# An attention, expert and feed-forward kernel on one core: the first token tile meets the first two experts by itself

## The chip, the core and the metric

The kernel is one program on one NeuronCore of a Trainium2 chip. TensorE (PE) multiplies matrices, VectorE (DVE), ScalarE (ACT) and GpSimd (POOL) do the rest, SyncE (SP) issues nearly all transfers. The metric is the time of one execution on the device in microseconds (us); less is better. The median of three runs before is 1221.71 us (1219.14 to 1221.81).

## What is computed

```python
def _attn_ref(q, k, v):                      # 2 x 8 heads, 576 positions, 64 wide
    scores = scale * np.matmul(q, k.transpose(0, 1, 3, 2))
    kth = np.partition(scores, -top_k, axis=-1)[..., -top_k:-top_k + 1]   # top_k = 32
    mask = scores >= kth
    ...
    return np.matmul(attn, v)

def _moe_ref(x, w_gate, w1, w2):             # 1152 tokens x 512, 8 experts, 1024 wide
    logits = x @ w_gate
    ...                                      # P: eight rounds of row and column sums over all tokens
    for e in range(E):
        h = np.maximum(x @ w1[e], 0.0)
        ye = h @ w2[e]
        out += P[:, e:e + 1] * ye

def _moe2_ref(x, w_in, w_out):               # 512 -> 2048 -> 512
    h = x @ w_in
    ...                                      # g = h * tanh(softplus(h))
    return g @ w_out
```

Attention gives 1152 tokens of 512 numbers; eight experts take every token, weighted by a gate that is normalised over all tokens; a last feed-forward part follows.

## The kernel before

**Tiles.** The tokens are nine tiles of 128 (t = 0 to 8). A unit of attention is one tile and one of its eight heads (t, h), so there are 72. The experts take the tiles in three chunks, `CHUNKS = [(0, 1), (2, 3), (4, 5, 6, 7, 8)]`. A pass (`ffn_pass`) is one expert on one chunk; it goes through eight pieces of the expert's weights (128 of the 1024 hidden columns each).

**Precision.** The experts' matmuls run on the rounded kind of float fp32r. Weights and tokens are split into a rounded part and the rest (`wh`, `wl`; `xh`, `xl`; `hh`, `hl`), and each product is three fp32r matmuls. For a piece, `load_piece` brings two 128x512 blocks (`wraw0`, `wraw1`, three buffers each), ACT rounds them and POOL (or DVE, later) subtracts. First matmuls `h` (12 for a chunk of two tiles, 256 columns each) go to PSUM under the tag `mm1` with two buffers; ACT makes `hh` from it, DVE makes `hl`, and both have to be done before the buffer is used again, so the `h` of piece f+2 waits for the `hl` of piece f. Second matmuls `y` (three of 512 columns for each tile) follow two pieces later (`LAG`).

**Attention unit.** PE makes scores `sc`, ACT copies them to `s`; DVE finds the 32nd largest number with four MAX8 (`top`) and three MATCH_REPLACE8 (`w`); ACT takes the exponential, DVE masks it and sums (`em`, `sm`; for the first 13 units POOL shares in that), DVE makes the reciprocal `r`, ACT scales `em`; PE transposes it (`tr`, `tr2`) and multiplies by the values (`pv`, once for two heads). When a tile is done its sums become `xh` and `xl`. Scores of tiles 2 and 3 and half of 5 and 6 are made early (`EARLY`) and kept in buffers or in DRAM (`away`).

**Order.** PE's order is written out by hand: the program runs generators, and what they yield in turn is PE's order. `attention()` runs alone until tile 1 is done. Then `moe_chunk(0)` and `moe_chunk(1)` are stepped (a step is one `h` or one `y` group), and attention advances by `RATE` units for each step after the first `HOLD`. After that chunk 2 and the last part run with PE alone to wait for. The order of the other engines is made by a scheduler at build time from priorities and stays fixed: each engine takes its instructions strictly in that order. The first MAX8 of each head of tile 2 is held behind the last reciprocal of tile 1:

```python
if i == 0 and t == CHUNKS[0][-1] + 1:
    if "ends" in live:
        after(top8, live["ends"])
```

Results of chunks 0 and 1 cannot be weighted before the gate is known, so `spill` copies `y` to SBUF (`ysp`, ACT and DVE in turn) and to DRAM.

## Time and profile before

| | |
|---|---|
| median of three runs | 1221.71 us |
| profiled execution | 1221.39 us |
| its span, first to last instruction | 1219.6 us |
| PE busy | 1168.7 us (96%) |
| DVE busy | 854.7 us (70%) |
| ACT / POOL busy | 660.2 us / 540.8 us |
| first matmul of the experts | 108.25 us |
| last head's transposes on PE | 521.16 us |
| first matmul of chunk 2 | 561.82 us |

1.8 us of the profiled execution lie outside its span. Ends of matmuls are modelled and matmuls overlap, so the rate of PE is read from the starts of matmuls that follow each other, not from their durations. The same holds for DVE, where the next instruction starts some 0.08 us before the one ahead is shown to end.

### The profile page before, as it was taken

Reading aid. Unit: us, or ns where it says so; the run is one execution under the profiler, and the core shown is the slowest. Engines: PE = TensorE matmul, PEld = TensorE weight load, DVE = VectorE, ACT = ScalarE, POOL = GpSimd, SP = SyncE. Lnnn points to the kernel's source line nnn. Section 1 sums busy time; section 2 is a strip of 40 time slices with the busy share of each in tenths; the row PEclk is TensorE's granted clock in tenths of the full one; section 3 lists DMA queues with packets and bytes.
Section 4 is the critical chain, followed back from the end, with each engine's and each line's share of the span. In section 5 each row is a group of like instructions: output and inputs, shape, how many; then the busy total and the mean of one; then the engine's idle time right before and its main releaser. Section 6 shows DMA issues by size and latency. Waiting matters only on the chain.

```text
span 1219.6 us, 21194 instructions
## 1 busy us (share of the span) xinstructions
PE 1168.7 (96%) x7459; PEld 1048.4 (86%) x7459; DVE 854.7 (70%) x1873; ACT 660.2 (54%) x1321; POOL 540.8 (44%) x424
## 2 busy tenths in 40 slices
PE   2677999999999999999999999999999999999998
PEld 2566888998989899899999999999999999999997
DVE  7999999999999999713656868677666633433221
ACT  6786777877777778654223333333333334554432
POOL 7844778877777877774112112121121122221210
PEclk9899999999999999999999999999999999999999
DMA  8434565576655555665235665656445332223201
GB/s 258 126 129 152 171 178 170 170 224 188 211 163 168 157 162 164 186 220 169 70 89 180 199 190 176 207 178 192 138 134 160 119 98 64 93 95 114 78 26 44
DMA packets 105114, 183.20 MB, mean 150 GB/s; under 512 B 14128, under 2 KB 24624, under 8 KB 105008
## 3 DMA queue, kind: packets, MB, share of 16 engines
q1 hardware_dynamic: 103712, 180.68, 47.6%
q8 instruction: 58, 0.95, 0.3%
q10 hardware_dynamic: 1296, 1.18, 0.3%
q14 instruction: 48, 0.39, 0.1%
HBM read 158.55 MB, written 23.27 MB: 149 GB/s over the span
## 4 chain that ended last, share of the span: by engine, by line
PE 86%; DVE 11%; DMA 1%; ACT 1%; issue 0%; POOL 0%; SPq 0%; POOLq 0%; ACTq 0%
PE h_c2e L619 18%; PE y_c2e L596 18%; PE h_d L619 8%; PE y_d L596 8%; PE y_c0e L596 7%; PE h_c0e L619 7%; PE h_c1e L619 6%; PE y_c1e L596 6%; DVE top L254 4%; DVE w L261 4%; PE pv L348 2%; PE tr L325 2%; PE sc L226 2%; PE pv L355 1%; DVE em L290 1%; DMA wraw_c0e<-in_wst_dram 1%
## 5 line engine op out<-in xcount | busy, mean ns | idle before, releaser
L522 POOL TENSOR_TENSOR wl_c2e<-wraw_c2e,wh_c2e 128x512 fp32r<-128x512 f32 x64 | 84.2, 1315 | 341.2 <-ACT wh_c2e L520 326.5
L522 POOL TENSOR_TENSOR wl_c0e<-wraw_c0e,wh_c0e 128x512 fp32r<-128x512 f32 x128 | 171.6, 1356 | 53.1 <-ACT wh_c0e L520 50.9
L522 POOL TENSOR_TENSOR wl_c1e<-wraw_c1e,wh_c1e 128x512 fp32r<-128x512 f32 x128 | 173.3, 1371 | 48.6 <-ACT wh_c1e L520 45.2
L520 ACT ACTIVATE wh_c2e<-wraw_c2e 128x512 fp32r<-128x512 f32 x128 | 80.8, 632 | 186.9 <-PE y_c2e L596 95.0
L254 DVE MAX8 top<-w 128x8 f32<-128x576 f32 x216 | 157.8, 747 | 0.8
L619 PE MATMUL h_c2e<-xh,wh_c2e 128*128 128x256 f32 (+1 forms) x512 | 158.3, 309 | 0.0
L619 PE MATMUL h_c2e<-xl,wh_c2e 128*128 128x256 f32 (+1 forms) x512 | 158.0, 309 | 0.0
L619 PE MATMUL h_c2e<-xh,wl_c2e 128*128 128x256 f32 (+1 forms) x512 | 157.8, 308 | 0.0
L538 DVE SCALAR_TENSOR_TENSOR hl_c2e<-h_c2e,hh_c2e 128x256 fp32r<-128x256 f32 (+1 forms) x128 | 62.5, 488 | 99.7 <-ACT hh_c2e L537 99.3
L596 PE MATMUL y_c2e<-wh_c2e,hh_c2e 128*128 128x512 f32 x320 | 126.0, 394 | 0.0
L596 PE MATMUL y_c2e<-wl_c2e,hh_c2e 128*128 128x512 f32 x320 | 125.9, 394 | 0.0
L596 PE MATMUL y_c2e<-wh_c2e,hl_c2e 128*128 128x512 f32 x320 | 125.2, 391 | 0.0
L522 POOL TENSOR_TENSOR wl_d<-wraw_d,wh_d 128x512 fp32r<-128x512 f32 x32 | 41.5, 1297 | 160.2 <-ACT wh_d L520 160.2
L520 ACT ACTIVATE wh_c0e<-wraw_c0e 128x512 fp32r<-128x512 f32 x128 | 80.5, 629 | 52.9 <-PE y_c0e L596 21.0
L261 DVE MATCH_REPLACE8 w<-top,w 128x576 f32<-128x576 f32 x144 | 106.4, 740 | 0.0
L557 DVE TENSOR_TENSOR hl_d<-mg_d,hh_d 128x256 fp32r<-128x256 f32 x64 | 38.5, 602 | 91.7 <-ACT hh_d L556 91.7
L520 ACT ACTIVATE wh_c1e<-wraw_c1e 128x512 fp32r<-128x512 f32 x128 | 80.3, 629 | 40.4 <-PE y_c1e L596 16.4
L619 PEld LDWEIGHTS h_c2e<-xh,wh_c2e 128*128 128x128 f32 x512 | 96.2, 188 | 2.5
L619 PEld LDWEIGHTS h_c2e<-xl,wh_c2e 128*128 128x128 f32 x512 | 96.1, 188 | 2.3
L619 PEld LDWEIGHTS h_c2e<-xh,wl_c2e 128*128 128x128 f32 x512 | 96.8, 189 | 0.0
L226 PE MATMUL sc<-ks,q 128*128 128x288 f32 x320 | 63.1, 330 | 26.0 <-ACT early L239 8.2
L537 ACT ACTIVATE hh_c2e<-h_c2e 128x256 fp32r<-128x256 f32 (+1 forms) x128 | 54.8, 428 | 55.3 <-PE h_c2e L619 53.0
(170 smaller groups left out, 3352.8 us busy)
## 6 DMA issues: line engine op xcount, KB each, us to landing
wraw_c0e<-in_wst_dram SPq DMA_DIRECT2D x128, 256.0 KB, 3.0
wraw_c1e<-in_wst_dram SPq DMA_DIRECT2D x128, 256.0 KB, 3.0
wraw_c2e<-in_wst_dram SPq DMA_DIRECT2D x128, 256.0 KB, 3.0
cx<-in_w_dram SPq DMA_DIRECT2D x32, 512.0 KB, 4.2
wraw_d<-w SPq DMA_DIRECT2D x64, 256.0 KB, 2.6
yd<-ysp SPq DMA_DIRECT2D x32, 256.0 KB, 3.6
yb<-yd SPq DMA_DIRECT2D x32, 256.0 KB, 3.2
w<-cc SPq DMA_DIRECT2D x32, 256.0 KB, 3.5
```

What stands on the lines that cost most here:

```text
L226: nc.tensor.matmul(halves[half], q[:, h % HG, :], ks[b, h][:, half * HS : (half + 1) * HS], start=(i == 0), stop=(i == len(terms) - 1),)
L254: top8 = nc.vector.max(g, src)
L261: nc.vector.match_replace(w, g, src, NEG)
L325: nc.tensor.transpose(tr[:, c, :], em[:, j * D + c * P :][:, :P], ident)
L348: nc.tensor.matmul(pv[i * D : (i + 1) * D, pair, c0:c1], vmain[b, pair][:, i, c, :], live["at", i][:, c, c0:c1], start=(c == 0), stop=False,)
L520: nc.scalar.activation(hi, raw, AF.Copy)
L522: eng.tensor_sub(lo, raw, hi)
L537: nc.scalar.activation(h, ps, AF.Relu)
L538: live["hl"] = nc.vector.scalar_tensor_tensor(l, ps, 0.0, h, op0=ALU.max, op1=ALU.subtract)
L557: nc.vector.tensor_sub(l, g, h)
L596: nc.tensor.matmul(y, h[:, j * P : (j + 1) * P], w, start=(f == 0 and k == 0), stop=(f == nf - 1 and k == 2),)
L619: nc.tensor.matmul(ps, w[:, c * P : (c + 1) * P], x[:, c, c0 : c0 + m], start=(k == 0), stop=(k == 3 * NC - 1),)
```

## The change

Tile 0 and experts 0 and 1 are taken out of the passes of chunk 0. A new generator, `alone(0, e)`, multiplies tile 0 by the unsplit weights in full precision (plain 32-bit floats, `wraw0` and `wraw1` straight from the transfer, no rounding, no subtraction): for a piece, four matmuls `h_a` of 128 columns, one ReLU on ACT, one matmul `y_a` of 512 columns. It is stepped beside tile 1's attention, from the moment at which tile 0 is done, at 4.8 steps for each unit. Chunk 0 and chunk 1 then run experts 2 to 7 as before, and two passes of the three tiles 1, 2 and 3 (384 columns) take experts 0 and 1 at the end of chunk 1 (`LateRelu`); the third tile's `y` stands in the PSUM tile of the scores (`sc`). `xh` and `xl` of chunks 0 and 1 become one tile each, so two early scores that lay there go to DRAM too (16 in place of 14). Tile 1's transposes use one PSUM bank in place of two. `RATE` becomes 0.29.

```diff
--- before.py
+++ after.py
@@ -47,7 +47,8 @@
 POOL_UNITS = 13
 EARLY = [(t, h) for t in (2, 3) for h in range(H)] + [(t, h) for t in (5, 6) for h in range(HG)]
 EARLY_FROM, EARLY_PER_STEP = 5, 2
-HOLD, RATE = 8, 0.25
+HOLD, RATE = 8, 0.29
+ALONE, ALONE_RATE = 2, 4.8
 FILL_FROM = 11
 
 
@@ -126,18 +127,23 @@
     xh, xl = {}, {}
 
     def x_tiles(i):
         if i not in xh:
-            xp = xlast if i == len(CHUNKS) - 1 else xfirst
-            n = P * len(CHUNKS[i])
-            xh[i] = xp.tile([P, NC, n], F32R, name=f"xh{i}", tag=f"xh{i}")
-            xl[i] = xp.tile([P, NC, n], F32R, name=f"xl{i}", tag=f"xl{i}")
+            ends = i == len(CHUNKS) - 1
+            xp, tiles = (xlast, CHUNKS[-1]) if ends else (xfirst, CHUNKS[0] + CHUNKS[1])
+            both = [xp.tile([P, NC, P * len(tiles)], F32R, name=f"{k}{i}", tag=f"{k}{i}") for k in ("xh", "xl")]
+            for j in [i] if ends else (0, 1):
+                at = P * tiles.index(CHUNKS[j][0])
+                xh[j], xl[j] = (x[:, :, at : at + P * len(CHUNKS[j])] for x in both)
+            if not ends:
+                xh["late"], xl["late"] = (x[:, :, P:] for x in both)
         return xh[i], xl[i]
 
     place = {t: (i, j) for i, c in enumerate(CHUNKS) for j, t in enumerate(c)}
 
     def groups(n):
 
-        return [(0, n)] if n <= 256 else [(0, 256), (256, n - 256)]
+        return [(0, n)] if n <= 384 else [(0, 256), (256, n - 256)]
 
     ps_b = wq = None
 
@@ -307,7 +313,7 @@
 
     def turned(t, i, name):
 
-        if t <= CHUNKS[0][-1] and i % 2:
+        if t < CHUNKS[0][-1] and i % 2:
             bank = ps_m.tile([P, 512], F32, tag="mm2", name=name, bufs=2)
         else:
             bank = ps_a.tile([P, 512], F32, tag="tr", name=name)
@@ -362,6 +368,10 @@
                     nc.scalar.activation(hi, pv[:, pair, :], AF.Copy)
                     nc.vector.tensor_sub(lo, pv[:, pair, :], hi)
             elif h == H - 1:
+                if t == 0:
+                    live["x"] = yp.tile([P, NC, P], F32, tag="ysp", name="x_alone")
+                    with st("first"):
+                        nc.scalar.activation(live["x"], pv, AF.Copy)
                 hi, lo = (x[:, :, i * P : (i + 1) * P] for x in x_tiles(ci))
                 nc.scalar.activation(hi, pv, AF.Copy)
                 nc.vector.tensor_sub(lo, pv, hi)
@@ -428,18 +438,16 @@
         def early(t, h):
 
             k = EARLY.index((t, h))
-            if k < 2:
-                x = xfirst.tile([P, S], F32, tag=("xh1", "xl1")[k], name=f"early{k}")
-            elif k < 10:
-                name = ("xh2", "xl2")[(k - 2) // 4]
-                if (k - 2) % 4 == 0:
+            if k < 8:
+                name = ("xh2", "xl2")[k // 4]
+                if k % 4 == 0:
                     stores[name] = xlast.tile([P, 4, S], F32, tag=name, name=f"early_{name}")
-                x = stores[name][:, (k - 2) % 4, :]
+                x = stores[name][:, k % 4, :]
             else:
                 with st("attn"):
                     x = sp.tile([P, S], F32, tag="away", name=f"early{k}", bufs=2)
             yield from scores(t, h, x)
-            if k >= 10:
+            if k >= 8:
                 with st("attn"):
                     away[t, h] = dram.tile([P, S], F32, tag=f"away_{t}_{h}", name=f"away_{t}_{h}")
                     nc.sync.dma_start(away[t, h], live.pop(("s", t, h)))
@@ -539,6 +547,23 @@
 
         later = ()
 
+    class LateRelu(Relu):
+        def __init__(self, name, n):
+            self.hh = qp.tile([P, n], F32R, tag="q1", name=f"hh_{name}", bufs=3)
+            self.hl = qp.tile([P, n], F32R, tag="q2", name=f"hl_{name}", bufs=3)
+    class Plain:
+        lag = 1
+        def __init__(self, name):
+            self.h = hp.tile([P, P], F32, tag="hh", name=f"h_{name}")
+        later = ()
     class Mish:
 
 
@@ -590,7 +615,10 @@
         def second(f, act, w2):
             with st("moe"):
                 if f == 0:
-                    ys.extend(bank2(f"y_{tag}_{t}") for t in tiles)
+                    third = ps_b is None and len(tiles) > 2
+                    ys.extend(bank2(f"y_{tag}_{t}") for t in tiles[: 2 if third else None])
+                    if third:
+                        ys.append(ps_a.tile([P, 2, 512], F32, tag="sc", name=f"y_{tag}_{tiles[2]}")[:, 0, :])
                 for j, y in enumerate(ys):
                     for k, (h, w) in enumerate(((act.hh, w2[0]), (act.hh, w2[1]), (act.hl, w2[0]))):
                         nc.tensor.matmul(
@@ -651,22 +679,71 @@
         spilled.append((t, e, d))
 
     def moe_chunk(ci):
-        for e in range(E):
+        rounds = [(e, CHUNKS[ci], x_tiles(ci), Relu) for e in range(ALONE if ci < 2 else 0, E)]
+        if ci == 1:
+            tiles = (CHUNKS[0] + CHUNKS[1])[1:]
+            rounds += [(e, tiles, (xh["late"], xl["late"]), LateRelu) for e in range(ALONE)]
+        for e, tiles, x, act_class in rounds:
             put = spill if ci in SPILLED else combine
             yield from ffn_pass(
                 f"c{ci}e{e}",
-                CHUNKS[ci],
+                tiles,
                 [wst[p] for p in range(e * EP, (e + 1) * EP)],
-                *x_tiles(ci),
-                Relu,
+                *x,
+                act_class,
                 lambda t, y, e=e, put=put: put(t, e, y),
             )
 
+    def alone(t, e):
+        ys = []
+        def second(f, act, w2):
+            with st("moe"):
+                if f == 0:
+                    ys.append(bank2(f"y_a{e}_{t}"))
+                nc.tensor.matmul(ys[0], act.h, w2, start=(f == 0), stop=(f == EP - 1))
+            if f == EP - 1:
+                with st("evict"):
+                    spill(t, e, ys[0])
+        for f in range(EP):
+            p = wst[e * EP + f]
+            with st("moe"):
+                raw = []
+                for a in range(2):
+                    raw.append(wp.tile([P, DM], F32, tag=f"wraw{a}", name=f"wraw{a}_a{e}_{f}", bufs=3))
+                    nc.sync.dma_start(raw[a], p[:, a * DM : (a + 1) * DM])
+                ps = ps_m.tile([P, 512], F32, tag="mm1", name=f"h_a{e}_{f}", bufs=2)[:, :P]
+                for c in range(NC):
+                    nc.tensor.matmul(
+                        ps, raw[0][:, c * P : (c + 1) * P], live["x"][:, c, :], start=(c == 0), stop=(c == NC - 1)
+                    )
+            act = Plain(f"a{e}_{f}")
+            with st("first"):
+                nc.scalar.activation(act.h, ps, AF.Relu)
+            yield
+            pending.append(Job(act, partial(second, f, act, raw[1])))
+            while len(pending) > pending[0].act.lag:
+                pending.pop(0).second()
+                yield
 
     at = attention()
-    for _ in at:
+    apart = chain(*(alone(0, e) for e in range(ALONE)), flush())
+    done, since = 0, None
+    for pos in at:
+        if "done" in live:
+            since = since or pos
+            while done < ALONE_RATE * (pos - since):
+                next(apart, None)
+                done += 1
         if live.get("done") == CHUNKS[0][-1]:
             break
+    for _ in apart:
+        pass
     mo = chain(moe_chunk(0), moe_chunk(1), flush())
     begin = pos = CHUNKS[0][-1] * H + H + AHEAD + 2
     for i, _ in enumerate(mo):
```

The built programs show what this does to the order. First, PE beside tile 1's attention, where names are tile and head (`sc_1_6` is scores of tile 1, head 6; `pv_1` the value sums of tile 1; `y_a0_0` and `h_a0_3` are expert 0 on tile 0). Before, from the scores of head 6 to those of head 7:

```order
L226 MATMUL sc_1_6_880<-ks_0_6_241,q2_1_1_0_593 128x288
L325 MATMUL tr_1_1_906<-ident_102,em_1_0_681 128x128 x4
L336 MATMUL tr2_1_1_913<-ident_102,em_1_0_681 128x128
...
L355 MATMUL pv_1_917<-at2_1_1_915,vt_0_0_154 128x128
...
L226 MATMUL sc_1_7_951<-ks_0_7_278,q2_1_1_0_593 128x288
L325 MATMUL tr_1_2_982<-ident_102,em_1_2_835 128x128 x4
```

And now:

```order
L232 MATMUL sc_1_6_922<-ks_0_6_241,q2_1_1_0_597 128x288
L721 MATMUL h_a0_3_933<-x_alone_796,wraw0_a0_3_929 128x128 x4
L331 MATMUL tr_1_1_959<-ident_102,em_1_0_685 128x128 x4
L707 MATMUL y_a0_0_853<-wraw1_a0_2_884,h_a0_2_891 128x512
L721 MATMUL h_a0_4_971<-x_alone_796,wraw0_a0_4_967 128x128 x4
L342 MATMUL tr2_1_1_978<-ident_102,em_1_0_685 128x128
L707 MATMUL y_a0_0_853<-wraw1_a0_3_931,h_a0_3_938 128x512
...
L361 MATMUL pv_1_983<-at2_1_1_980,vt_0_0_154 128x128
L721 MATMUL h_a0_5_999<-x_alone_796,wraw0_a0_5_995 128x128 x4
...
L232 MATMUL sc_1_7_1028<-ks_0_7_278,q2_1_1_0_597 128x288
L707 MATMUL y_a0_0_853<-wraw1_a0_4_969,h_a0_4_976 128x512
L721 MATMUL h_a0_6_1040<-x_alone_796,wraw0_a0_6_1036 128x128 x4
```

The value sums of the first pair and the scores of head 7 now stand behind first and second matmuls of six and five pieces of expert 0, counted from the end of tile 0.

Second, DVE after the last reciprocal of tile 1 (`r_1_7`), up to the first `hl` of the experts. Before:

```order
L300 RECIPROCAL r_1_7_1142<-r_1_7_1142 128x1
L254 MAX top_2_0_1127<-early0_321 128x8
L254 MAX top_2_1_1153<-early1_330 128x8
...
L363 TENSOR_TENSOR xl0_793<-pv_1_917,xh0_792 128x128
L261 MATCH_REPLACE w_2_0_1128<-top_2_0_1127,w_2_0_1128 128x576
L261 MATCH_REPLACE w_2_1_1154<-top_2_1_1153,w_2_1_1154 128x576
L254 MAX top_2_0_1127<-w_2_0_1128 128x8
L538 SCALAR_TENSOR_TENSOR hl_c0e0_0_1208<-h_c0e0_0_0_1209,hh_c0e0_0_1207 128x256
```

And now:

```order
L306 RECIPROCAL r_1_7_1308<-r_1_7_1308 128x1
L260 MAX top_2_0_1293<-early_xh2_321 128x8
L260 MAX top_2_1_1331<-early_xh2_321 128x8
...
L296 SCALAR_TENSOR_TENSOR em_2_0_1345,sm_2_0_1344<-early_xh2_321,top_2_0_1293,e_2_0_1302 128x576
L676 COPY ysp_0_1_1384<-y_a1_0_1194 128x512
L369 TENSOR_TENSOR xl0_799<-pv_1_983,xh0_798 128x128
...
L305 TENSOR_SCALAR r_2_2_1724<-sm_2_2_1721 128x1
L260 MAX top_2_6_2008<-early_xl2_453 128x8
L546 SCALAR_TENSOR_TENSOR hl_c0e2_0_1416<-h_c0e2_0_0_1417,hh_c0e2_0_1415 128x256
```

Before, 16 rows stand between the two; now 52: 19 MAX8, 14 MATCH_REPLACE8, four masks, one spill copy, three `xl` and eleven small ones. From the `xl` of tile 0 to `r_1_7` there were 17 MAX8, 12 MATCH_REPLACE8, two compares and four `xl`; now there are 18, 15, three and two.

Third, DVE where the heads of tile 4 begin (tiles 0 to 3 have their scores early or are done). Before:

```order
L538 SCALAR_TENSOR_TENSOR hl_c0e3_6_2721<-h_c0e3_6_0_2722,hh_c0e3_6_2720 128x256
L254 MAX top_3_6_2760<-w_3_6_2761 128x8
L254 MAX top_3_7_2867<-w_3_7_2868 128x8
L254 MAX top_4_0_3041<-s_4_0_2746 128x8
L290 SCALAR_TENSOR_TENSOR em_3_6_2881,sm_3_6_2880<-s_3_6_2525,top_3_6_2760,e_3_6_2769 128x576
L290 SCALAR_TENSOR_TENSOR em_3_6_2881,sm_3_7_3054<-s_3_7_2561,top_3_7_2867,e_3_7_2876 128x576
L261 MATCH_REPLACE w_4_0_3042<-top_4_0_3041,s_4_0_2746 128x576
```

And now:

```order
L305 TENSOR_SCALAR r_3_6_2953<-sm_3_6_2950 128x1
L305 TENSOR_SCALAR r_3_7_3116<-sm_3_7_3114 128x1
L306 RECIPROCAL r_3_6_2953<-r_3_6_2953 128x1
L306 RECIPROCAL r_3_7_3116<-r_3_7_3116 128x1
L546 SCALAR_TENSOR_TENSOR hl_c0e5_0_2698<-h_c0e5_0_0_2699,hh_c0e5_0_2697 128x256
L546 SCALAR_TENSOR_TENSOR hl_c0e5_1_2733<-h_c0e5_1_0_2734,hh_c0e5_1_2732 128x256
L676 COPY ysp_1_4_2763<-y_c0e4_1_2350 128x512
L546 SCALAR_TENSOR_TENSOR hl_c0e5_2_2780<-h_c0e5_2_0_2781,hh_c0e5_2_2779 128x256
L260 MAX top_4_0_3101<-s_4_0_2822 128x8
```

Before, the first head of tile 4 lies among work of tile 3; now three `hl` and a copy stand ahead of it with no attention between them. On PE the scores `sc_4_0` stand where they stood, between the transposes of heads 3 and 4 of tile 3; DVE now has all of tile 3 behind it by then, where before two masks of tile 3 came after.

## Rows read from the trace of the kernel before

**Rows 1.** The page: busy time of two engines, and 40 slices of the span.

```profile
PE 1168.7 (96%) x7459; PEld 1048.4 (86%) x7459; DVE 854.7 (70%) x1873; ACT 660.2 (54%) x1321; POOL 540.8 (44%) x424
...
PE   2677999999999999999999999999999999999998
...
DVE  7999999999999999713656868677666633433221
```

**Rows 2.** The page: the chain that ended last, shares by engine.

```profile
PE 86%; DVE 11%; DMA 1%; ACT 1%; issue 0%; POOL 0%; SPq 0%; POOLq 0%; ACTq 0%
```

**Rows 3.** Busy time by stretch: PE, PEld, DVE, ACT, POOL, clock, DMA share, GB/s.

```profile
76.50:108.25 31.75, 22.32 (x163) 17.44 (x162) 31.68 (x86) 25.68 (x60) 10.91 (x10) 0.95 0.55 174
104.50:509.10 404.60, 400.69 (x2980) 358.41 (x2981) 397.72 (x972) 304.06 (x592) 313.55 (x234) 1.00 0.57 175
540.00:560.00 20.00, 20.00 (x131) 18.12 (x130) 6.01 (x12) 11.93 (x24) 17.73 (x15) 1.00 0.78 239
```

**Rows 4.** DVE, then PE, in order of time: last head of attention, then chunk 2.

```profile
507.94 0.82 DVE L290 SCALAR_TENSOR_TENSOR em<-s,top,e 128x576 f32<-128x576 f32 x1
...
508.99 0.17 DVE L300 RECIPROCAL r<-r 128x1 f32<-128x1 f32 x1
...
519.33 0.60 PE L325 MATMUL tr<-ident,em 128*128 128x128 f32 x4
519.69 0.48 PE L596 MATMUL y_c1e<-wh_c1e,hh_c1e 128*128 128x512 f32 x1
...
521.16 0.60 PE L325 MATMUL tr<-ident,em 128*128 128x128 f32 x4
...
561.82 0.28 PE L619 MATMUL h_c2e<-xh,wh_c2e 128*128 128x256 f32 x1
```

**Rows 5.** PE in order of time, a `y` group, an `h` group, the next `y`.

```profile
117.22 0.39 PE L596 MATMUL y_c0e<-wh_c0e,hh_c0e 128*128 128x512 f32 x1
...
118.59 0.28 PE L619 MATMUL h_c0e<-xh,wh_c0e 128*128 128x256 f32 x1
...
119.98 0.39 PE L596 MATMUL y_c0e<-wh_c0e,hh_c0e 128*128 128x512 f32 x1
```

**Rows 6.** The chain in order of time, chunk 2: 12 `h` of 256 columns, 12 of 384.

```profile
615.71 3.53 PE h_c2e L619 x24
```

**Rows 7.** PE in order of time: end of tile 0's, then of tile 1's attention.

```profile
76.23 0.49 PE L355 MATMUL pv<-at,vt 128*128 128x128 f32 x2
...
108.00 0.49 PE L355 MATMUL pv<-at,vt 128*128 128x128 f32 x2
108.25 0.36 PE L619 MATMUL h_c0e<-xh,wh_c0e 128*128 128x256 f32 x1
```

**Rows 8.** ACT's copies of 128x128, all: count | busy us, mean ns | idle before.

```profile
L339 ACT ACTIVATE at<-tr 128x128 f32<-128x128 f32 x36 | 9.6, 268 | 0.0
```

**Rows 9.** Transfers between 76 and 109 us.

```profile
DMA packets 4948, 5.56 MB, mean 168 GB/s; under 512 B 2384, under 2 KB 2896, under 8 KB 4944
```

**Rows 10.** DVE in order of time: from tile 0's end to the first `hl`.

```profile
78.90 0.67 DVE L367 TENSOR_TENSOR xl<-pv,xh 128x512 fp32r<-128x512 f32 x1
...
104.47 0.16 DVE L300 RECIPROCAL r<-r 128x1 f32<-128x1 f32 x1
104.55 1.40 DVE L254 MAX8 top<-early 128x8 f32<-128x576 f32 x2
105.86 1.40 DVE L254 MAX8 top<-early_xh 128x8 f32<-128x576 f32 x2
107.18 0.07 DVE L261 MATCH_VALUE_LOAD w<-top,early 128x8 f32 x1
107.24 0.74 DVE L261 MATCH_REPLACE8 w<-top,early 128x576 f32<-128x576 f32 x1
107.90 0.14 DVE L271 TENSOR_SCALAR nb<-top 128x1 f32<-128x1 f32 x1
...
112.51 0.40 DVE L538 SCALAR_TENSOR_TENSOR hl_c0e<-h_c0e,hh_c0e 128x256 fp32r<-128x256 f32 x1
```

**Rows 11.** DVE's `hl` (L538) alone, in the long stretch of attention.

```profile
104.50:509.10 404.60, 45.39 (x111) 1.00 0.57 175
```

**Rows 12.** The mask's line: count, shortest, median and longest duration in ns.

```profile
L290 DVE SCALAR_TENSOR_TENSOR em<-s,top,e x49: 798/865/1891, 95.5 to 507.9; 128x576 f32<-128x576 f32 x49
```

**Rows 13.** Groups of instructions: DVE's MAX8 on scores, and what it waited for.

```profile
L254 DVE MAX8 top<-s 128x8 f32<-128x576 f32 x62 | 46.5, 750 | 6.0 <-ACT s L235 5.7 <-DMA s<-away 0.2
```

## The prediction

> **What bounds the kernel now.** I read the page first. PE is busy in nine tenths or more of every slice from the fifth on, and DVE in nine tenths or more of slices 2 to 15 [rows 1]. The chain that ended last gives PE 86% and DVE 11% [rows 2]: one engine nearly throughout, and the other ahead of it. Two stretches settle what that means [rows 3]. Between 104.5 and 509.1 us, from the first MAX8 of tile 2 to the last reciprocal, DVE is busy 397.7 of 404.6 us and PE 400.7: both are full, so neither has room to take work from the other's shortage. From 540 us on PE is full and DVE busy 6 of 20. Third, the ends [rows 4]: DVE is through with attention at 509.2 us, PE makes the last transposes at 521.2 and begins chunk 2 at 561.8. So DVE is 10 us ahead at that point, and PE sets the end. Before 108.25 us it is the other way: between 76.5 and 108.25 DVE is busy 31.7 of 31.75 us, PE at most 22.3 [rows 3]. The gap there is what the change wants to fill.
>
> All sums below are made against the profiled execution: 1221.39 us, span 1219.6, 1.8 outside. The median of the runs is 1221.71, 0.3 above. I take 0.3% (3.7 us) as what a measurement here can tell from no change.
>
> **What the change takes out.** A `y` group of two tiles lasts 1.37 us and an `h` group of 256 columns 1.39, start to start [rows 5], so a two-tile piece costs 2.76. In chunk 2 the 24 `h` of 256 and 384 columns last 3.53 [rows 6], which leaves 2.14 for 384 columns; nine `y` at 0.228 are 2.06, so a three-tile piece costs 4.20. Out go 32 two-tile pieces (88.3 us), in come 16 three-tile ones (67.2): **21.1 us less PE work** behind the start of the experts. The 384-column form gains nothing by itself. What is saved is tile 0's share.
>
> **What it adds beside tile 1.** Per piece four plain 32-bit matmuls of 128 columns and one of 512. The trace has the first: `pv` of 128x128 (two records) starts at 108.00 and the next matmul at 108.25 [rows 7], 0.25 us. The 512-column one it does not have: at least 0.23 us (the fp32r form), at most four times 0.25; I take 1.0, since it is the same kind of number. A piece is 2.0 us (1.2 to 2.0), 16 are 32 us (20 to 32). The Trainium skill's page FP8 and Floating Point Precision, TensorE Precision Notes, says that true FP32 takes four passes through the array. No run here shows that for 512 columns; by it the `y_a` would be 4 x 0.228 = 0.91 us and the 16 pieces 30.6 us.
>
> Tile 1's own PE work there is at most 22.3 us [rows 3], and less, since ends are modelled; I take 18. Tile 0 ends at 76.5 [rows 7], so the experts' split passes can start on PE at 76.5 + 18 + 32 = 126.5, with some waits **128** (117 with the low price, 140 if nothing overlaps), against 108.25. On ACT come 16 copies of 128x128 (0.27 us each [rows 8]) and two larger ones, 5.5 us on top of 25.7 busy [rows 3]: covered, because the stretch grows to some 50 us. If it were not covered, it would cost those 5.5 us. The transfers: 5.56 MB were moved in that stretch [rows 9], and 13 more pieces of 0.52 MB after three preloaded ones make 12.4 MB; at 239 GB/s, the rate of a full stretch [rows 3], 52 us, to 128.5. That is just hidden by PE's own 128; two more early scores to DRAM are in that noise. SP issues in order, and some of the weights stand behind fetches of scores that wait for a buffer which a mask of tile 1 frees, so they can't run ahead of DVE.
>
> **What it moves on DVE, which decides.** DVE's order from tile 0's `xl` to the last reciprocal of tile 1 took 78.90 to 104.63 us without a pause [rows 10]. The new order has one MAX8 (0.655 each, from the starts at 104.55 and 105.86), three MATCH_REPLACE8 with their load (0.72, 107.18 to 107.90) and a compare (under 0.7) more there, and two small `xl` fewer: 3.0 us, because the `xl` of tile 0 now comes sooner in the order and still has to wait for the same PE work. So tile 2 begins on DVE at **107.6** (104.6 if that slack is found elsewhere, 115 if the 11 us of new PE work ahead of head 7's scores are not covered by the 9 us in which PE idled).
>
> Then 52 rows stand ahead of the first `hl`: 19 x 0.655 + 14 x 0.72 + 4 masks of 0.8 + some 2 = 27.7 us, to 135.3. Before it was 112.5. The third `h` group waits for that `hl` and stands 2.8 us behind the first, so PE in effect starts at 132.9, not at 128: a shift of 24.7 us against 21.1 saved, **+3.6 us** from this alone. What is late next is every `y` behind it.
>
> **The DVE sum.** From tile 2 on DVE has the same 56 heads. Its 397.7 us fall by eleven `hl` (111 [rows 11] against 100 by the same head, at 0.41 less 0.08 of overlap), less 0.6 for four wider ones, and by one copy of 0.6: 3.6. The masks: shortest 0.80 us, median 0.87, longest 1.89 [rows 12], so something holds them up. POOL is busy 313.6 of these 404.6 us [rows 3]. The Trainium skill's page SBUF — State Buffer, SBUF: two separate sides, says that DVE and GpSimd share a port pair, and a DVE operation with two SBUF inputs and a GpSimd one that reads SBUF shut each other out for a whole instruction. The spread of the masks agrees; that POOL causes it is not shown by the rows. With a tenth fewer subtractions in the stretch the masks might lose a tenth of their excess, 1.5 us (0 to 14, if all ran at their shortest). So DVE needs 392.6 us.
>
> Idle time: 6.9 us before, of which MAX8 on fresh scores waited 5.7 over the whole kernel [rows 13]. DVE's 158 rows from that first `hl` to `top_4_0` sum to 80 us, to 215; PE's work from the third `h` to the end of `sc_4_0` to 84, to 219.5: DVE, planned further ahead than it was, waits 4 us at tile 4. With half of the rest, 7.6 us idle (2 to 14). Attention ends on DVE at 107.6 + 392.6 + 7.6 = 507.8; 2 us later the last transposes can go. Behind them stand 12 of the 112 `h` groups and 14 of the 112 `y` groups, all of three tiles, 12 x 2.14 + 14 x 2.06 and 1.5 of attention, 56 us: chunk 2 begins at 565.8, where it was 561.8. **+4.0 us**, 1225.4 in all. From there both kernels are the same PE work, and I take no difference. The two sums meet: PE starts as much later as it has less to do, and then DVE, for which the pace of 0.29 is too fast, keeps it waiting. The saved PE time goes into waits for DVE.
>
> **Rivals.**
>
> *Faster: DVE turns out lighter, and PE's work decides.* If `hl` is never late, chunk 2 begins 19.8 us later for the start at 128 less 21.1 saved; with a start at 125 it is 4.4 us sooner, with the low price of the plain matmuls 12. For it speaks that DVE was 10 us ahead at the end and that masks can run at 0.80, worth 14 us. Against it: DVE has no gap between 76.5 and 108.25, and the 52 rows are its own work. It decides if the first `hl` comes before 130. The SBUF page's rule would, if the masks all ran at their shortest, take the same side. Time 1209 to 1218, say 1216; chance 0.17.
>
> *No difference.* The first `hl` at 134, and no excess of DVE later: 1221 to 1225, say 1223. 0.25.
>
> *Much slower: the lonely experts starve.* Their weights come at 174 GB/s, the rate of that stretch [rows 3], not 239: 12.4 MB then last 71 us, PE starts at 147 and in effect 14 us later than I take it. It sets in under 220 GB/s. For it: SP's order and a depth of three buffers. Against: 239 GB/s was held in a full stretch. 1230 to 1240; 0.13.
>
> **How the numbers follow.** The forecast, DVE sets the pace up to the end of attention, has 0.45: 1225.4, from 1221 to 1231 by the bounds of the idle time (2 to 14) and of 107.6. A third of it lies within 0.3%. Together: faster 0.17, same 0.36 (0.21 of the second rival, 0.15 of the forecast), slower 0.47 (0.30, 0.13 and 0.04). The range reaches down to 1215 into the faster case and up to 1235 into the starving one, which leaves out about a tenth on each side.
>
> **What would show it.** In the new profile: the first `y_a` as long as 1.0 us, start to start; the first split `h` near 128 and the third at 135 to 136, waiting for DVE `hl`; MAX8 of tile 2 from 107 to 108; PE idle 8 us or more in all between its start at 128 and the last transposes, for DVE's `hl` at first and later for `em` before `tr`, where the long stretch of before has 3.9; DVE idle near tile 4; DVE through with attention at 505 to 510; chunk 2 at 564 to 568. Wrong would be: a PE without waits up to the late passes, or a start of tile 2 on DVE past 112.

## The result, and the profile after

The changed kernel takes 1233.33 us (median of 4 runs, 1232.09 to 1234.48), the kernel before on the same chip 1221.76: a ratio of 1.0095, 95% interval 1.0072 to 1.0117. It is slower by 11.6 us, where 3.7 were forecast; the range of 1215 to 1235 holds it. The profiled span is 1232.7 us, 13.1 more than before.

The page after: busy time, the slices of PE and DVE, the granted clock, and the shares of the chain that ended last.

```profile
PE 1175.9 (95%) x7379; PEld 1048.3 (85%) x7379; DVE 843.8 (68%) x1857; ACT 644.7 (52%) x1290; POOL 491.6 (40%) x392
...
PE   3789899999999999999999999999999999999998
...
DVE  7999899699999999612556777767666633433221
...
PEclk9899899999999999999999999999999999999999
...
PE 62%; DMA 1%; DVE 0%; ACT 0%; issue 0%; ACTq 0%
```

Against [rows 1], PE and DVE have an 8 in slice 5 (123 to 154 us) and DVE a 6 in slice 8 (216 to 247 us), where both had nines. This chain, unlike [rows 2], is followed back through 63% of the span only, to 448 us, and says next to nothing of attention. The waits have to be read stretch by stretch.

Busy time by stretch, columns as in [rows 3]: the alone work, attention from the first MAX8 of tile 2 to the last reciprocal, and a stretch of late passes.

```profile
75.08:126.46 51.38, 46.07 (x309) 34.20 (x309) 50.72 (x135) 36.60 (x83) 15.33 (x14) 1.00 0.82 264
103.49:509.28 405.79, 388.86 (x2854) 342.76 (x2851) 387.21 (x959) 294.49 (x576) 283.02 (x217) 0.98 0.57 178
555.00:575.00 20.00, 20.00 (x100) 17.85 (x99) 4.39 (x8) 7.74 (x14) 8.28 (x7) 1.00 0.43 130
```

The long stretch lasts as long as before (405.8 and 404.6 us), but now both engines have gaps in it: DVE 18.6 us where it had 6.9, PE 16.9 where it had 3.9. Neither was the bound throughout. In the stretch of late passes (555 to 575 us) PE is full and DVE busy 4.4 of 20.

The end of attention, which answers to [rows 4]: DVE's last mask and reciprocal, then on PE the last transposes and chunk 2.

```profile
507.83 1.05 DVE L296 SCALAR_TENSOR_TENSOR em<-s,top,e 128x576 f32<-128x576 f32 x1
...
509.12 0.17 DVE L306 RECIPROCAL r<-r 128x1 f32<-128x1 f32 x1
...
520.17 0.60 PE L331 MATMUL tr<-ident,em 128*128 128x128 f32 x4
...
576.28 0.28 PE L647 MATMUL h_c2e<-xh,wh_c2e 128*128 128x256 f32 x1
```

Chunk 2 begins 14.5 us later than before; after it the two kernels differ by 1.4 us only (657.8 us to the end before, 656.4 after). So all of the loss is made ahead of chunk 2.

**A sum for PE.** From the first split `h` to chunk 2 I take off PE's waits (each idle time above 0.1 us) and half of the time that it ran at half the clock outside those waits; what is left is work. Before: 453.6 us, 2.5 of waits, none at half the clock, 451.0 of work. After: 449.8 us, 14.5 of waits, 10.4 at half the clock, 430.1 of work. So the change at chunk 2 is +18.2 (start at 126.46 where it was 108.25) - 20.9 (work) + 12.0 (waits) + 5.2 (clock) = +14.5. The forecast had the first two, 19.8 and 21.1; its +4.0 leaves 5.3 us for more waits, and it had no term for the clock.

PE's waits in that stretch: us in all, times, longest.

```profile
PE tr L331 <- ACT em L311: 5.7, 2, 2.9
PE h_c0e L647 <- ACT xh L368: 2.5, 1, 2.5
PE pv L361 <- ACT at L345: 2.3, 3, 1.5
PE h_c0e L647 <- DVE hl_c0e L546: 1.7, 1, 1.7
PE y_c1e L624 <- DVE ysp L676: 1.4, 1, 1.4
PE y_c0e L624 <- DVE nb L277: 1.4, 2, 1.0
PE tr L342 <- ACT at L334: 1.0, 1, 1.0
```

(1.5 of the `pv` row stand just ahead of the start, at 126.21.) No transfer is among them. The first `hl` is the small one; the largest are two waits for `em` in the middle of attention, which the forecast had only towards its end.

The start of the split passes on PE, in order of time, and then the granted clock around it (columns as above, the clock third from the right).

```profile
126.21 0.49 PE L361 MATMUL pv<-at,vt 128*128 128x128 f32 x2 [1.47 <-ACT at L345]
126.46 0.37 PE L647 MATMUL h_c0e<-xh,wh_c0e 128*128 128x256 f32 x1
...
130.19 0.58 PE L647 MATMUL h_c0e<-xh,wh_c0e 128*128 128x256 f32 x1 [2.45 <-ACT xh L368]
...
131.33 0.41 PE L647 MATMUL h_c0e<-xl,wh_c0e 128*128 128x256 f32 x1
131.54 0.41 PE L647 MATMUL h_c0e<-xh,wl_c0e 128*128 128x256 f32 x1
...
135.56 0.58 PE L647 MATMUL h_c0e<-xh,wh_c0e 128*128 128x256 f32 x1 [1.69 <-DVE hl_c0e L546]
```

```profile
120.00:126.40 6.40, 4.90 (x32) 2.91 (x31) 5.98 (x18) 4.34 (x9) 4.08 (x4) 1.00 0.71 213
128.70:138.90 10.20, 7.02 (x29) 6.59 (x30) 8.73 (x26) 5.91 (x13) 9.51 (x7) 0.50 0.70 234
139.00:149.00 10.00, 10.00 (x65) 8.98 (x65) 9.17 (x20) 7.18 (x14) 9.01 (x7) 1.00 0.56 173
```

Three waits of 5.6 us in all lie within 11 us. From 128.7 to 138.9 us, from within the second of them on, the granted clock is 0.50, which is 1.2 GHz: matmuls of 256 columns start 0.21 us apart there, and 0.116 at 2.4 GHz (12 in 1.39 us, [rows 5]).

### The profile page after: what moved, and what is told of

Read it like the earlier page. It is cut to its first block, busy times and chain, and to the rows that moved or that the text cites. A ratio compares the mean times of both kernels' runs of the same rounds, so it can differ in the third digit from the quotient of the medians.

```text
span 1232.7 us, 20940 instructions
## 1 busy us (share of the span) xinstructions
PE 1175.9 (95%) x7379; PEld 1048.3 (85%) x7379; DVE 843.8 (68%) x1857; ACT 644.7 (52%) x1290; POOL 491.6 (40%) x392
## 4 chain that ended last, share of the span: by engine, by line
PE 62%; DMA 1%; DVE 0%; ACT 0%; issue 0%; ACTq 0%
PE y_c2e L624 18%; PE h_c2e L647 18%; PE h_d L647 8%; PE y_d L624 8%; PE y_c1e L624 4%; PE h_c1e L647 4%; PE pv L354 0%; PE tr L331 0%; DMA yd<-ysp 0%; PE x2t L800 0%; PE sc L232 0%; PE pv L361 0%; DMA wraw_c1e<-in_wst_dram 0%; PE cs L500 0%; PE lt L399 0%; ACT wh_c2e L528 0%
## 5 line engine op out<-in xcount | busy, mean ns | idle before, releaser
L530 POOL TENSOR_TENSOR wl_c1e<-wraw_c1e,wh_c1e 128x512 fp32r<-128x512 f32 x128 | 168.6, 1328 | 83.9 <-ACT wh_c1e L528 83.7
L530 POOL TENSOR_TENSOR wl_c0e<-wraw_c0e,wh_c0e 128x512 fp32r<-128x512 f32 x96 | 127.4, 1341 | 50.7 <-ACT wh_c0e L528 48.4
L528 ACT ACTIVATE wh_c0e<-wraw_c0e 128x512 fp32r<-128x512 f32 x96 | 60.1, 629 | 42.7 <-PE y_c0e L624 15.0
```

Of the source, the lines that this page charges most:

```text
L528: nc.scalar.activation(hi, raw, AF.Copy)
L530: eng.tensor_sub(lo, raw, hi)
```

## The experiments

All are edits of the changed kernel unless it is said otherwise. The table has the same sum for each (us; "start" is the first split `h`, "half" the time at half the clock outside waits, the ratio is to the kernel before on the same chip). The columns from "start" on are read from one profiled execution of each, and that can lie some us from the median: in run 3 it took 1226.61 us, where the median is 1231.09, and in run 6 the executions spread from 1229.04 to 1240.69.

| run | median | ratio, 95% interval | start | chunk 2 | waits | half | work |
|---|---|---|---|---|---|---|---|
| before | 1221.76 | | 108.2 | 561.8 | 2.5 | 0 | 451.0 |
| changed | 1233.33 | 1.0072 to 1.0117 | 126.5 | 576.3 | 14.5 | 10.4 | 430.1 |
| 1 tail | 1228.55 | 1.0026 to 1.0055 | 124.9 | 572.8 | 13.4 | 6.3 | 431.3 |
| 2 one expert | 1228.64 | 1.0031 to 1.0063 | 116.9 | 571.3 | 8.2 | 12.4 | 439.9 |
| 3 one piece each | 1231.09 | 1.0042 to 1.0085 | 116.8 | 568.6 | 16.2 | 8.8 | 431.2 |
| 4 lighter DVE | 1224.13 | 1.0004 to 1.0027 | 125.8 | 566.2 | 7.5 | 5.7 | 430.0 |
| 5 HOLD 0, RATE 0.27 | 1224.55 | 1.0011 to 1.0034 | 126.7 | 566.2 | 5.9 | 6.3 | 430.4 |
| 6 AHEAD 3 | 1232.80 | 1.0076 to 1.0127 | 124.8 | 574.1 | 14.1 | 6.7 | 431.8 |
| 7 before, lighter DVE | 1220.60 | 0.9984 to 1.0004 | 107.6 | 562.9 | 2.6 | 0 | 452.8 |
| 8 tail, HOLD 0, RATE 0.27 | 1220.87 | 0.9990 to 1.0012 | 122.2 | 562.8 | 8.2 | 3.4 | 430.6 |
| 9 HOLD 0, RATE 0.29 | 1235.62 | 1.0109 to 1.0137 | 127.6 | 578.5 | 14.0 | 9.8 | 431.9 |
| 10 before, HOLD 0, RATE 0.24 | 1230.54 | 1.0067 to 1.0094 | 107.8 | 573.6 | 10.9 | 4.8 | 452.5 |
| 11 one expert, HOLD 0 | 1224.73 | 1.0021 to 1.0047 | 112.1 | 567.3 | 11.2 | 3.0 | 442.5 |
| 12 one expert, HOLD 6 | 1218.74 | 0.9973 to 0.9993 | 112.2 | 559.4 | 5.7 | 0 | 441.4 |

The last column shows that the sum holds: 451.0 to 452.8 with no expert alone, 439.9 to 442.5 with one, 430.0 to 431.9 with two. Work is what the number of experts makes it; the kernels differ in start, waits and clock.

**1, the tail.**

```diff
-ALONE, ALONE_RATE = 2, 4.8
+ALONE, ALONE_RATE = 2, 3.4
```

> ALONE_RATE 3.4 in place of 4.8 in the changed kernel: the same alone pieces, but three and a half of them now stand on PE behind the last values of tile 1, where PE waited for xh (2.5 us), then for the first hl (1.7 us), at the half clock for 10 us. Theory W (PE's own waits and its slow stretch, once lost, stay lost up to chunk 2): the start is covered, DVE's wait of 3.1 us at the last xl goes too, and 5 to 8 us come back: 1225 to 1228 us, chunk 2 at 568 to 571. Theory D (DVE's sum sets the end of attention, as predicted): only DVE's own 3.1 us come back, 1230 us, chunk 2 at 573. Theory T (too early an attention, the pace of 0.29, makes the waits later on): 1231 to 1234, since the waits between 160 and 420 us stay or grow.

1228.55. PE no longer waits for `xh`, though now 3.3 us for `hl`; the time at half the clock falls from 10.4 to 6.3 us, and DVE's last reciprocal comes 3.5 us sooner. That is 4.8 us by the medians and 6.6 by the ratios (the kernel before took 1222.99 on that chip), while chunk 2 at 572.8 in the trace is theory D's number. The run does not part D from W; the two waits for `em` (5.7 us) are there unchanged.

**2, one expert alone.**

```diff
-HOLD, RATE = 8, 0.29
-ALONE, ALONE_RATE = 2, 4.8
+HOLD, RATE = 8, 0.27
+ALONE, ALONE_RATE = 1, 2.4
```

> ALONE 1 in place of 2 in the changed kernel, at half the alone rate (2.4) and a pace of 0.27: one expert takes tile 0 alone and one three-tile pass follows. Alone work falls from 29.3 to 14.7 us, of which PE's waits before 108 us cover some 10; saved are 10.5 us. Theory W: split passes start at 113 to 115, chunk 2 at 561.8 + 6 - 10.5 and half of the waits of the changed kernel (8): 564 to 566, 1224 to 1226 us; if the waits do not come, 1216 to 1218, below both kernels. Theory D: DVE has one compare and 5 hl more than with two experts and the same start at 103 to 105, so attention ends at 509 or later and the time is 1230 or more.

1228.64, between the theories. Half of the alone work brought the start down by 9.5 us, and 9.8 of saved work went; but PE still waits 4.1 us for `em` and 4.0 ahead of the third `h`, and loses 6.2 to the clock.

**3, one piece of eight.**

```diff
...
-            if f == EP - 1:
+            if f == 0:
...
-        for f in range(EP):
+        for f in range(1):
```

> The alone passes of the changed kernel do only the first of eight pieces each (14 of 16 alone pieces and their weights are left out, so tile 0 lacks most of experts 0 and 1); all else stays. Some 25.6 us of PE work beside tile 1 go. Theory W: the split passes start at 108 to 111, chunk 2 comes as much earlier as they do less the waits that the earlier start adds, 561 to 567, 1218 to 1224 us. Theory D: DVE's work from tile 2 on is the same and starts no sooner than 102, so attention ends on DVE at 505 to 508, and the time falls by no more than 4 us, to 1229 to 1233. If PE set the pace alone: chunk 2 at 558, 1214.

1231.09 (1226.61 to 1233.83; the profiled run is the lowest). Theory D has the size: with some 25.6 us of PE's work gone (14 of the 16 pieces) the time falls by 2 (by 6.7 in the profiled run). But in the trace, which is of the fastest execution, 7.7 of the 9.6 us by which the start is earlier reach chunk 2, as theory W has it; so the run does not decide. And the start is a surprise: 116.8, not 108 to 111. PE's transposes of tile 1 in that trace:

```profile
108.87 0.66 PE L331 MATMUL tr<-ident,em 128*128 128x128 f32 x4 [0.69 <-ACT at L334]
110.62 0.33 PE L342 MATMUL tr<-ident,em 128*128 128x128 f32 x1 [1.09 <-ACT at L334]
...
113.91 0.66 PE L331 MATMUL tr<-ident,em 128*128 128x128 f32 x4 [1.08 <-ACT at L334]
115.31 0.33 PE L342 MATMUL tr<-ident,em 128*128 128x128 f32 x1 [0.75 <-ACT at L334]
```

With one PSUM bank these transposes wait until ACT has copied the one before, 3.6 us in all here. That is a cost of the change that the forecast left out. Another 3.8 us of the late start are DVE's: its last reciprocal of tile 1 comes at 108.27, where it came at 104.47 before. In the changed kernel only 0.3 us of PE's waits before the start are of this kind, so there the alone matmuls that lie between cover it.

**4 and 7, a lighter DVE in both kernels.**

```diff
-            for i in range(TOPK // 8):
+            rounds = TOPK // 8 if t < 2 else 3
+            for i in range(rounds):
...
```

> The changed kernel with three rounds of MAX8 in place of four for tiles 2 to 8 (the threshold is the 24th number there and not the 32nd; one MAX8 and one MATCH_REPLACE8 of each of 56 heads are left out, 77 us of DVE work). DVE can't be late between 140 and 510 us any more. Theory W: all of PE's waits for DVE behind 139 us (10.4 us) and the slow clock beside them (1.5 us) go, and some 1.5 us at the first hl; the waits for xh and the start stay: chunk 2 at 562 to 565, 1219 to 1222 us, level with the kernel before. Theory D: PE waited for DVE for more than that, and the time falls under 1215. Theory T (PE's waits come from the order, not from the amount of DVE work): less than 5 us come back, 1228 to 1233.

> The kernel before with three rounds of MAX8 in place of four for tiles 2 to 8 (threshold at the 24th number; one MAX8 and one MATCH_REPLACE8 of each of 56 heads are left out). If DVE costs the kernel before nothing but PE's 2.5 us of waits, as its trace shows: chunk 2 at 558 to 560, 1217 to 1220 us, and the changed kernel with the same lighter DVE (chunk 2 at 566.2) stands 6 to 8 us behind it. If DVE holds that kernel up more than its waits show: under 1214.

1224.13 and 1220.60. DVE's busy time falls by 58 us in the changed kernel (843.8 to 785.7) and by 67 in the kernel before (854.7 to 787.6), less than the 77 counted. The kernel before gains nothing that can be told (its interval holds 1); the changed kernel gains 9.2. So DVE costs the one nothing that shows and the other most of what it lost, and the two stand 3.5 us apart, where 6 to 8 were expected. The 1224.13 is near W's number (1219 to 1222), and far from the fall under 1215 that D asked for and from T's 1228. What is left between the two at chunk 2, 3.3 us, is 18.2 (start) - 22.8 (work) + 4.9 (waits, mostly for ACT) + 2.9 (clock).

**5, 9 and 10, the pace.**

```diff
-HOLD, RATE = 8, 0.29
+HOLD, RATE = 0, 0.27
```

> HOLD 0 and RATE 0.27 in place of 8 and 0.29 in the changed kernel: attention goes on beside the experts from the first step, eight steps earlier at the start and as late at the end. Theory S (DVE's own idle time of 17 us, 10 of it between 216 and 243 us for tile 4's scores and hl, sets the end): tile 4's scores come some 10 us sooner, DVE idles 7 to 9 us, its last reciprocal comes at 500 to 502, chunk 2 at 567 to 570, 1224 to 1227 us. Theory P (PE's own waits set it, DVE's idle time does not count): the transposes come sooner too and wait for em more than the 5.7 us of the changed kernel; PE's waits stay at 14 us or more, 1232 to 1237 us.

1224.55: theory S has the number. Its reason does not hold: DVE idles 11.9 us and not 7 to 9, and its last reciprocal comes at 506.0, 3.1 us sooner and not 7 to 9, yet chunk 2 comes 10.1 sooner. It is PE's waits that fell, from 14.5 to 5.9:

```profile
PE tr L331 <- ACT em L311: 2.6, 2, 1.8
PE h_c0e L647 <- ACT xh L368: 2.2, 1, 2.2
```

The ninth run parts the two numbers (HOLD 0, RATE 0.29).

> HOLD 0 alone in the changed kernel, RATE stays 0.29, so attention stands eight steps earlier all through and ends eight steps earlier. It parts the two numbers that the fifth run changed together. Theory H (attention started too late, so DVE ran dry at tile 4): DVE idles 10 us or less, 1224 to 1227 us as in the fifth run. Theory R (the pace of 0.29 leaves PE 6.4 us for a head, of which DVE needs 7.0, so PE must wait for em): PE catches up sooner, waits 15 us or more in all, 1230 to 1236 us.

1235.62, theory R, though PE's waits are 14.0 us and not 15. DVE was through at 501.3, 7.8 us sooner than in the changed kernel and with 8.2 us of idle time where that has 18.6, and chunk 2 came 2.2 us later. This is the plainest evidence against the step "DVE's end sets the end". From run 5 this run differs in RATE alone: 0.27 in place of 0.29 is worth 11 us, a ratio of 1.0022 in place of 1.0123. PE's largest waits there:

```profile
PE tr L331 <- ACT em L311: 6.8, 2, 3.7
PE pv L361 <- ACT at L345: 2.4, 1, 2.4
PE tr L342 <- ACT at L334: 2.0, 2, 1.5
```

RATE 0.27 with HOLD 8 was not tried with two experts alone: the scores of the last heads would come behind a late pass whose third `y` holds their PSUM tile. Then the tenth, the same earlier begin in the kernel before (HOLD 0, RATE 0.24).

> The kernel before with HOLD 0 and RATE 0.24 in place of 8 and 0.25 (attention begins beside the experts eight steps earlier and ends at the same step), the edit that brought the changed kernel 9 us. If that gain was a wait that only the change had made: no difference, 1219 to 1223 us. If it is there for any version: 1213 to 1217 us.

1230.54, neither: 9.5 us worse than the kernel before on that chip. One wait makes most of it, at 123.5 us, for the first `em` of tile 2:

```profile
PE tr L325 <- ACT em L305: 7.3, 1, 7.3
```

There PE starts at 107.8, and with HOLD 0 it comes to tile 2's transposes before DVE has its heads. In the changed kernel PE starts 19 us later, and the same eight steps are no longer needed. So the gain of the fifth run belongs to the changed kernel: its HOLD and RATE did not fit its start and its number of steps.

**6, scores further ahead (AHEAD 3 in place of 2).**

> AHEAD 3 in place of 2 in the changed kernel: the scores run one head further ahead of the rest of a unit on PE, some 6.4 us; the transposes keep their place among the experts. Theory S: DVE's waits for tile 4 fall by 5 to 8 us, the last reciprocal comes at 502 to 504, and the time is 1225 to 1228. Theory P: PE's waits for em and hl stay, 1231 to 1234.

1232.80, theory P. DVE's last reciprocal came 3.7 us sooner, its idle time nearly stayed (17.3 us), PE's waits too (14.1). It was not the scores' place in the order. But the waits moved: the two for `em` now stand at 476 and 491 us (3.2 us in all) and no longer in tiles 4 and 5, while others for `hl`, `r` and `nb` grew.

**8, tail and pace together.**

> The edits of the first and the fifth run of this list together (ALONE_RATE 3.4, HOLD 0, RATE 0.27) in the changed kernel. Theory S: both gains add, chunk 2 at 562 to 566, 1219 to 1224 us, no worse than the kernel before. Theory P: as the first alone, 1228 to 1232 us.

1220.87, as S has it, and level with the kernel before.

**11 and 12, one expert at the old pace.** From run 2: `RATE = 0.25`, `ALONE_RATE = 1.9`, HOLD 0 and then 6, and tile 1's transposes on both `mm2` banks again:

```diff
-        if t < CHUNKS[0][-1] and i % 2:
+        if t == CHUNKS[0][-1] or t < CHUNKS[0][-1] and i % 2:
...
-                    ys.append(bank2(f"y_a{e}_{t}"))
+                    ys.append(bank1(f"y_a{e}_{t}"))
```

> The changed kernel with one expert alone (ALONE 1, ALONE_RATE 1.9), HOLD 0, RATE 0.25, and both mm2 banks for the transposes of tile 1 (y_a takes the tr bank). Alone work is 14.7 us, saved are 10.5. Theory R and S (PE's saving counts if the pace fits DVE's 7 us a head): split passes start at 110 to 114, PE waits 5 us, chunk 2 at 556 to 560, 1214 to 1218 us, below both kernels. Theory D (DVE's sum sets it): the last reciprocal at 503 to 506 and chunk 2 at 562 to 565, 1219 to 1223, the same as before.

1224.73, above both ranges. The start is 112.1 as forecast (116.9 in run 2), but PE waits 4.7 us for the first `em` of tile 2 at 126, the wait of the tenth run.

> The eleventh run (one expert alone, both mm2 banks for tile 1's transposes, RATE 0.25) with HOLD 6 in place of 0: attention beside the experts begins six steps (8 us) later, which is more than the 4.7 us that PE waited there for the first em of tile 2. Theory R with the sum of PE (start of the split passes + 440.8 us of work up to chunk 2 + PE's waits + half of the time at the half clock): start 112, that wait and the slow stretch gone, 5 to 7 us of waits left, chunk 2 at 557 to 561, 1215 to 1219 us, under the kernel before. Theory D (DVE's sum sets the end; its last reciprocal came at 515.7 in the eleventh run): the wait turns up elsewhere, 1223 to 1226 us.

1218.74 against 1221.02 on the same chip, 0.9973 to 0.9993: that wait is gone, the sum of PE held, and this version is faster than the kernel before by 0.17% (and than the changed kernel by 1.1%, by the ratios). It was measured on one chip only. PE's waits from the start to chunk 2, and the clock of its page:

```profile
PE tr L331 <- ACT at L334: 2.4, 3, 1.8
PE h_c0e L647 <- DVE hl_c0e L546: 1.9, 1, 1.9
PE h_c0e L647 <- DVE r L305: 1.3, 1, 1.3
PE tr L331 <- ACT lg L410: 0.2, 1, 0.2
```

```profile
PEclk9999999999999999999999999999999999999999
```

DVE's last reciprocal is at 514.3 there, 5.2 us later than in the changed kernel, and chunk 2 is 16.9 sooner. Theory D falls with that.

## Why the prediction was right, and where its size was off

**Right: what comes out and goes in.** 21.1 us of PE work forecast, 20.9 measured, and the runs with one expert show half of it. A `y_a` is two records, and from one to the next piece:

```profile
119.67 1.02 PE L707 MATMUL y_a<-wraw_a,h_a 128*128 128x512 f32 x2
120.53 1.05 PE L721 MATMUL h_a<-x_alone,wraw_a 128*128 128x128 f32 x8
```

0.86 us, where I took 1.0. The Trainium skill's page FP8 and Floating Point Precision, TensorE Precision Notes, has true FP32 take four passes through the array; the forecast's estimate from that, 0.91, is nearer to the trace than my choice. The 16 pieces took 29.3 us, start to start, where 32 were forecast.

**Right: the start.** 126.46 where 128 stood. The 29.3 us of alone work moved the start by 18.2, so 11 were covered by PE's gaps.

**Right, by two errors: the first `hl`.** It came at 135.11, where 135.3 stood. But DVE began tile 2 at once and not after 107.6, and lost the time later, when the last `xl` of tile 1 stood in its order and PE had not yet made the values that it reads:

```profile
103.41 0.16 DVE L306 RECIPROCAL r<-r 128x1 f32<-128x1 f32 x1
103.49 1.40 DVE L260 MAX8 top<-early_xh 128x8 f32<-128x576 f32 x2
...
130.17 0.29 DVE L369 TENSOR_TENSOR xl<-pv,xh 128x128 fp32r<-128x128 f32 x1 [3.06 <-ACT xh L368]
...
135.11 0.40 DVE L546 SCALAR_TENSOR_TENSOR hl_c0e<-h_c0e,hh_c0e 128x256 fp32r<-128x256 f32 x1
```

4.1 us gained at the start of tile 2 and 3.1 lost at that `xl` nearly cancel: the number is luck in part. The wait that the forecast feared ahead of tile 2 ("115 if ... are not covered") came at the `xl`, and smaller.

**Right as a sum, wrong in its parts: DVE's end.** 507.8 forecast, 508.8 measured for the reciprocal of the head before the last, 509.1 for the last. Busy time was 387.2, not 392.6, and idle time 18.6, not 7.6 (bounds 2 to 14). The busy time fell by 10.5 us where 5.1 were counted. The `hl` fell by 5.6 where I had 3.0 (97 of them lie in the stretch, not 100), and the masks by 3.0 (62.95 to 59.95) where I took 1.5; the last 1.3 are not traced:

```profile
103.49:509.28 405.79, 39.81 (x97) 0.98 0.57 178
```

POOL's busy time fell from 313.6 to 283.0 there. The Trainium skill's page SBUF — State Buffer, SBUF: two separate sides, has a DVE operation with two SBUF inputs and a GpSimd one that reads SBUF lock each other out of a port pair that they share. Shorter masks beside less POOL work have the direction of that; that POOL is the cause is not shown by any run here. Of the idle time, 9.8 us lie between 216 and 243 us at tile 4, where the forecast had 4. DVE's largest waits in the whole stretch:

```profile
DVE hl_c0e L546 <- ACT hh_c0e L545: 6.5, 7, 2.2
DVE top L260 <- ACT s L241: 5.5, 3, 3.6
DVE xl L369 <- ACT xh L368: 3.1, 1, 3.1
```

**The step that failed: "Attention ends on DVE at ... 507.8; 2 us later the last transposes can go", and with it "The two sums meet".** The transposes came at 520.2, 11 us behind DVE, as they had been 12 behind it before [rows 4]. The forecast let that lead of DVE shrink to 2 us; it did not. The 56 us after that were right (56.1), so 9 of the 10.5 us by which chunk 2 was missed are there. DVE's end is not what PE waits for. The last place where DVE holds PE in this kernel is the last head of tile 5, 150 us earlier:

```profile
299.70 0.14 DVE L306 RECIPROCAL r<-r 128x1 f32<-128x1 f32 x1
300.70 0.55 PE L331 MATMUL tr<-ident,em 128*128 128x128 f32 x3 [2.93 <-ACT em L311]
...
355.87 0.14 DVE L306 RECIPROCAL r<-r 128x1 f32<-128x1 f32 x1
...
356.87 0.55 PE L331 MATMUL tr<-ident,em 128*128 128x128 f32 x3 [2.81 <-ACT em L311]
```

These are heads (4, 7) and (5, 7). Their transposes stand 1.0 us behind DVE's reciprocals, the smallest distance in this trace from tile 2 on, while a head later the distance is 13 us. Before it was 2.6 and 3.3 us: these were the tight places already, with 1.6 and 2.3 us to spare. From (5, 7) on PE goes through to chunk 2 with 1.9 us of waits and 3.4 at half the clock, so two numbers decide: when DVE lets it through there, and how much of the experts' work is then still ahead.

| | `tr` of (5, 7) | from there to chunk 2 |
|---|---|---|
| before | 347.4 | 214.4 |
| changed | 356.9 | 219.4 |
| run 9 (HOLD 0, RATE 0.29) | 346.7 | 231.8 |
| run 5 (HOLD 0, RATE 0.27) | 350.3 | 215.9 |
| run 12 (one expert, 0.25) | 353.4 | 206.0 |

That is what the pace does. A step of two tiles is 1.38 us of PE [rows 5], attention's own matmuls are 1.43 a head (80.3 us, start to start, over 56 heads), so at 0.29 PE takes 1.38/0.29 + 1.43 = 6.2 us for a head, at 0.27 6.5, at 0.25 7.0. DVE takes 387.2/56 = 6.9. At 0.29 PE runs into DVE at the tight places with fewer of the experts' steps done, and the late passes then stand alone after attention with DVE mostly idle. The forecast had this in a half sentence ("the pace of 0.29 is too fast") but put the wait at the end of attention and not at (4, 7) and (5, 7), and it had no term for the stretches at half the clock (5.2 us). These two places are not the same in every order: in run 6 PE waits for `em` in tile 8 instead, and its waits add up to 14.1 us where the changed kernel has 14.5. So it is the sum of the waits that counts and not one place.

**The rivals.** DVE lighter, PE decides: DVE was lighter (387.2 us against 392.6), and PE was still held. The starving experts: no. 13.57 MB came in the stretch at a mean of 264 GB/s, more than the 239 assumed, and PE waits for no weights. The time, 1233.33, is one of the starving case (1230 to 1240, chance 0.13) by another road: it lies above the forecast's own bounds of 1221 to 1231, and the range holds it only because it was drawn up to 1235 for weights that would starve. That much is luck.

Two readings of [rows 1] were off by a slice, and nothing rests on them: DVE is full up to slice 16 and not 15, and PE's last slice is an 8.

**What stays open.** How the 10.4 us of waits behind 139 us divide between pace, start and DVE's order of heads was not parted further. Runs 5 and 9 show that the pace moves them, run 4 that a lighter DVE takes most of them away. That the stretches at half the clock come from the waits is not shown either: they stand beside them.

## What to carry to other kernels

Where two engines run in fixed orders, do not set the later of two end times as the result: find the places at which one waits for the other, sum the waits up to the last of them, and add what is still ahead of the waiting one. When steps are merged into fewer, longer ones, a pace counted in steps has to be set anew against the other engine's time for a unit, and against the new start. Work slipped into an engine's gaps is free only up to the size of the gaps: here one expert fitted, at 0.17% less time, and two came out level at best (run 8).

## What the hardware showed that was not expected

Transfers: GB/s in 40 equal slices between 75 and 126.5 us.

```profile
GB/s 0 234 204 282 268 315 153 308 208 158 267 231 43 180 349 288 274 353 269 252 341 383 400 400 384 409 370 330 313 292 245 295 251 220 207 215 302 135 264 151
```

A full-looking stretch of before at 239 GB/s [rows 3] was no ceiling: in three slices of 1.3 us, among loads of 256 KB, 400 to 409 GB/s were moved here.

The clock: the granted clock fell to 1.2 GHz beside the waits at 126 to 136 us (10.2 us) and behind the one that ended at 356.87 (3.4 us, from 357.4 on), but not behind the one of nearly the same size that ended at 300.70. In the profiled execution of run 12, with no wait above 2 us from the start on, it did not fall there; its mean granted clock, 0.997, is the highest of the run's eleven executions (0.992 to 0.997), so others may have lost some. Here a wait of some 3 us was followed by 1.7 us lost to the clock in one place, and by nothing in another.
